# A radix-2 step in the channel transform of a fused attention and spectral-filter kernel

## The chip, the cores and the metric

The kernel runs on one core of one Trainium2 chip. The metric is the device time of one execution in microseconds (us).

## The reference

```python
x = A_x                                            # 1 x 2048 x 448, bf16
g = sigmoid((x * gate_w).sum(-1, keepdims=True))
q, k, v = heads(x @ A_wqkv)                        # 16 heads of 28
a = (softmax(q @ k.T * 28 ** -0.5) @ v) @ A_wo
X = rfft2(x)                                       # 2048 tokens x 225 frequencies
b = irfft2(X * (w_r + 1j * w_i))
out = g * a + (1 - g) * b
```

Both halves read A_x (B_x isn't used): attention over 16 heads, and a two-dimensional Fourier filter over tokens and channels. g mixes them for each token.

## The kernel before

**Attention.** Heads go in four groups of four; each head has a 32-row strip of the array. Queries are taken in four chunks of 512, so there are 16 (group, chunk) pairs, and 16 tiles of 128 keys each. A score matmul (K = 32 rows, 512 columns) gives one head's scores for one key tile. Two ways lead from there to the exponential. Most units go in pairs through psA or psB to ScalarE (L1032, 128x1024, 366 of them) into `ring`. The others (ND key tiles of each pair, 73 in all, four heads each) are done without ScalarE: VectorE turns the scores into the bit pattern of a bf16 power of two (L991, 292 of them, out of a `bg` bank into a `pd` tile), and GpSimd makes three more copies with shifted phase by an integer addition (L1001, INT64_ADD, 219 of them). Both kinds are then multiplied with the weighted values into the accumulator `pvb`, four matmuls side by side, one for each head (128x32 weights, 512 columns). There are nine `pd` tiles (NPD); one is free again when its `pvb` matmuls have read it.

**The spectral part** (`background`, L1249) is spread between the attention's instructions. Tokens are numbered so that partition p, tile t hold token 16p + t. Its stages:

- `fwd(t)` (L1269), 16 times: the channel transform of 128 tokens. The transposed tokens xT, in four chunks of channels (128, 128, 128, 65), are multiplied with the cosine and sine matrix Bd (450 columns: 225 frequencies, real and imaginary) into one `bg` bank, four accumulating matmuls, each split into four column tiles (`mm4`, L414). VectorE copies the bank to X1 (L1284).
- `fwd2(t)` (L1287): a 128-point transform over partitions with the matrix A, an eviction (L1296) and a DMA into the layout of the next stage (tile xtok, named UT there).
- `mid(g)`, 16 times (in `background`): the rest of the token transform as three `mm4` with the matrices CS (450, 225 and 225 columns), the product with the filter on VectorE (L1343 twice, then the two sums of SBUF tiles that give Z, L1348 and L1350), three `mm4` back and an eviction into UT (L1367).
- `inv(t)`, 16 times: a DMA brings the rows back to V2, four matmuls of 128 columns with A undo the 128-point transform, and VectorE multiplies with 1 - g, divided by g, into zt (L1388).
- `out_tile` (L1201) and `last_tile` (L1222), 16 together: one bank collects four `mm4` of the inverse channel transform (zt with Binv, which lies in Bd's tile, 448 columns each; rows of 225 frequencies in two pieces of 113, real and imaginary) and four `mm4` of the heads' output with `wo` (448 columns, in the tiles wpq and wpk). The eviction multiplies with g, and a DMA writes 128 tokens out. Four of these tiles come after the last exponential.

Projections of q, k and v (`proj_group`, `v_block`, `x_block`, `w_block`) are spread in the same way.

**What sets the order.** Every engine's instructions stand in one total order that is written out: the string TABLE holds, compressed, the number of each operation in the order of emission, with a second list that gives each use of a rotating bank one of three `bg` banks. `Sched.run` (L273) emits them so, and `pin` (L300) keeps that order on each engine. Numbers from 60000 on would be filler matmuls; this table has none. The planner's costs (the first arguments of `pe`, `dve`, `pool`) and due times are left in the code but decide nothing at run time.

**The shared port.** VectorE operations that take their operands from SBUF are marked `lk`: `ported` (L309) makes the next GpSimd instruction of the order wait for them. Of these are the squares of q and k (L745), the normalisation (L1176), Z (L1348, L1350) and the phase-weighted values (L886).

All matmuls are recorded under line 426, the helper `mm`; all DMAs under 401.

Of the kernel before, what the change touches and what calls it, by code (L numbers as in the profile page):

```python
# [13 lines left out]
BF16 = mybir.dt.bfloat16  # L14
# [8 lines left out]
F2 = 2 * F  # L23
NT, J, P = 16, 8, 128
FS, FN = (0, 112), 113
# [6 lines left out]
NPD, DKT = 9, 5  # L32
FILL0 = 60000
DUE_P = 4.0
TABLE = (
    "eNoN1oNyHloUQOF9tI//NGmjKqlt27Zt27Zt27Zt27Zt+95nWDPfLA1VAIBALAiFMGgAbSAcIiASPMSGOBAX4kF8iAID0dABEkBCSASJIQkk"
    "hWSggIKEFMAgAAhpIQTSgICaYKEGdIRsUB1SQUpIDtUgHaSHypAFUoOD7JADMkEGyAnBkBEyQ1YoBjEhBlSEXFAcSkApKA1BkB9KQm7IA4td"
    "GegNVaEcVIKy0ALyQj4oDF2gAMQk5aEg1IEKUAiKwBIXi4SSp1AUnkEYCScRpAdEktjkObyAl/AKXsMbiENyYC6MS+KRtxCfRJGcGE0SkIQk"
    "EXkHK2AlrILVsAbWQmKyDtZDT0hCJsBEmASTIQ/egSmwAWpDbtwId+Ee3IdNsBm2wFbYBtthB0yD6ZAXH8AMmAmzYDbMgbkwDx5CQ9jmdkJd"
    "mA8cFkAt2AULYREshkewBJZCE3gM+bAARrvd0BSewDJoBvlxDyyHvbAP3kNLSEoK4gf4CI1hP3SFA/AJPkM3KIKF8CDUhx1uKrSFwpiMJCeH"  # L40
    "oDmE6S9QFA9DCnIEjkJKUgyPwVcI1cXxG0wnM0gqMhBmkuNQCltDCUxNTkBJ7AxVSTUyi6Qh1UlprEHSklbQCU5CGUxH0pOyWJNkIBlJJlIO"
    "T8FpOANn4RychwtwEcrjbFIBs5Ih0B4yk2wkO8lBcpJc5DvkJpfgMuQhFTEvScAqYT6y012Bq5CfJGTXYLO7DgVIQVKIVMYbcBOykFtwG6pg"
    "YVKElCFVsSgpS4qRavgDfkJx8guSsepYAyN1claO1MTy5DdUILUwWtfGcB2b1cHYOg4bTerBH6iL9bAXJGIVyRiSmI0l3aE+jiOLXBLWAIEQ"
    "QgkjDXE84aQRCIJEEkU0aYTtIIIZ8g8sScoi2V9wxJPGGCBRLiULIk0wBqlEgklc3RTj62YYxkJICZJUN8d6rgVWJqVJfVeFtMSSpIFL58JZ"
    "K0zFGrrWmN41cnFZCtYGM7h4LLnO6NpiatYOM7lolky3x4Q6DUvPOmBCV4rUIolcYtcRM7BOGJ+lZUlcOtYZE+kumJEldVG6K8bR3bAwy8Qi"
    "dGLdA7tjEVacRbFcLIlOoXthT8zBEujemJul1CVYPJ2TZWF5WCqdl2VmfbAe6Yv1STbWD1Pr7KwBaUj6YyNSlBVjAzCrzqIHYkE2CAdjMZeV"
    "FXfZdCE2BEu42iSNHoql2DCsQwqwzDqHHo4lXSVWkpVyI7AuyalHYhFdhlVm5Vg+VpblZ6MwrS7N8uvRmFuPwfIsl07mxmJ1Ng6TuxRuPKZ0"
    "FdgEzKcL6YpsIg6CSZjKZdDpdTVWg2XXRfVknIKNSV3WjOXVefRULKanYQFdlU3Heqwzqc1mYBfSlczEOmwWdiNldEfWnczGOTgXm7PCuqCu"
    "yWqxediJldLNyXxsQRZgCV1aN2ELsSmrwhZhS9KKLMYl2IK1JvVZS1ZOl9QNWW63FNuyZdiOLcfiuqxegeV1PpdOr8T8rhHL41ZhLd2YFXAZ"
    "9Wos6Aq5NdiZdWFtWAW9FnuS+nod9mC9SD29HjfgUteEZNIbsQHrySrq3qSS3oR9yGasrWvoLdjMbcW+pClp7rZhe9bCdWD9SEO9HZuRlm4H"  # L50
    "9mOtXFPdn3VjO7GOHsx2YWvWWFfVNfVu3IN92BDWQu/F5ro768v2YWXdi/VmbUk7sh8P4EjWnoxiHchBbKlHQ0cylB3Cuno8tGKHsZw7gsNY"
    "XjecjWDlXQV3FHuQiu4YjmOdSCXXSY9lx7GBPoFDSRN9EgeyUziBTWSt9Wkcz7rqRrqLHkZSuzTuDJ7DtC6bG07O4giS3Y0kg1gOl9OdxwuY"
    "y61gK1l73ZVNJAPYJVzGLuJy1k5fxklkFWtDruBksppNIcPgKo5m1XQzPZWMYTPZNWylr2M3PYlNYTewg57FJrOp7Cb2J7ewmruNHXUbPYHM"
    "Z2NgALmDbfVdnM6quxlsAbuHS9hSVsPdx866pnuA3fVisoQsJcvIQ5zNlpNa7hH20EP1AD2NDNOD9BMcRR7jXDaHbWVVtGdj9Rj9FLexZ7ib"
    "bHF7yF6yj9wjz/E+eUAekmnsEZlD9pMD5CB5TJ6Qp+QQ6amfkcPkCHlOjpJjZAh5QQaRZe44mccC7AQ5SU6RV3iavMCXOFAvZCP1XDKPrCKL"
    "yGoyn6wga8hL8oqsJevIa1xPXpMNZCPZRHrpN6S6foNvyWayhWwl28hb3E52kJ3kHS4gi9l69o5M0EP0B9zMNrD3uIsMJMP1YP0Rt7A17BOu"
    "Y3tYZfcZp+sqbrT+govYATZO72UT9VdcyxaSwWQj+4bj3Cj9Hfvpg2y828T66Ml6gvuBp9lJdortZL/wDPuJQWy8HqEnuml6kvuN8/Qf3MeG"
    "ub84S//DXWw/286Gu91shAOZ2fUBIrO4wo7KHWyKzuqYPM4m6SLuBBvpRjkuhSzqrrC5+iqbqlHeZVJeYDP0RXaYHWFztJKz9T12iGlpZHxa"
    "2pVxvbWVR1kULetmaierOi9DWDQ9xubrleQsS0ADMiYLku1cQrpAx5DnWXtX29VxwfI+6+AesMEQIju6mPIS6+TW6FhyhV6pr7FQeYacJefI"
    "eRIm++rL7AK5SC6RyyRc3mbX2Tl2hVwl18gtdoddJzfITRIhb5HbJFLeIf3cKn2XxJY7dRy5UH8ii3R/956s13Flf/2KLdOvWTy51T1kA9xA"  # L60
    "FyUXuvhyg37Etuho2c19IAnkGzbIbdPLXUK53a3VS3UM9pEkki9Yd/eEvWQ3WA+XWPZ0SWRSeVC/Zb3cOv2ZJZPP2HO2Wm/VyWVd94WlkE/Z"
    "V7ZDT3Mp5WM23X1jN9kflkru0qnlDPeXpZGMz3Scz3KbdDqZVn5k79lm3dnt1enlUOjiMshP7DvbqD+wo3qJ/sEyykzyH9un37HMcrsG3tVl"
    "kYT/ZPt1Y5dVZpOGU75bW75HZ5f94Bc7pGOxHNLxnDKUHdCtXRP3m3mueC55TB/WuWWAa55HtnFBvK37TI7ovPK4jsklzye/kK8kv0ReQJ7Q"
    "sXgkD+EXdGx+TX8j30koLygLyWAexhO423q0Kywv6cR8jDupi8gRcEcXlVf1KZ2Ep+DFZAx+RV/UxWVKHs4juOAlZFM32I11l3VJGZ+Xkj9I"
    "PP5AP9ZD3GJdWkbxm7qMTMOf67IyLf9J4vKhrpyM5tf1L5KAl5cVZEL+myzXt3RFWUkm4ql4al5ZxuFJ+Sv9h1SR6fhf8lCf0VXlI93bpefV"
    "ZFZ+Qz/R1eU/0sfVkNl5X3dPJ+P3dU2ZmdeSL/RdnZzn4Nl4Jl5bznNZeB0529WVz/R8N8fVk6d1Ab7AFeSTXX2Zkc91b3QDOcXl5G/1WZ2Y"
    "NpS5eBKalE51yWgjmZxm4E1kEZ6bN5aF+GtdmL/U5zTQpzoPbyrz8WayKM/Pm0tC32lK3+vyvARvIRmtwFvKFe6DXulaSU5XudZyl1vtdjtB"
    "i/M17oduI/PytpKbdrIkF6a9LMX3uBAak8aiofSX3uv2uQ6ykwyjH/Unfdt1lP90BD2vI2kxHpvGoZ3lXx2XdpFlOTPlODVrXVfZTZbmSCUd"
    "Cftdd9lDluHrXGOu6EnXhGtqaE9ZhfeSv3Vvud590xtcH/lTV+Vf9UanjaV95QF32vWTm1xFXp834I7+0f3lKBgga/DK/K7zNIYJMwOlNDV5"
# [1370 lines left out]
```

## Time and profile before

| | |
|---|---|
| time, median of 3 runs | 384.12 us (384.02 to 384.2) |
| the profiled execution's own time | 384.64 us |
| its span | 382.8 us |
| granted TensorE clock | 0.999 |
| instructions | 12650 |

The span goes from the first to the last instruction; the time has 1.84 us around it. In rows of groups stand the line, engine, operation, tiles written and read, shapes and count, then busy time, mean duration in ns, and the idle time ahead of it with what ended it. In rows of a timeline stand start and duration in us and the count of merged instructions. In rows of stretches stand the stretch, its length, and the busy time of each engine with the number of instructions, then clock, DMA share and GB/s. PE is TensorE, PEld its weight loads, DVE VectorE, ACT ScalarE, POOL GpSimd.

### The profile page before, as it was taken

The page shows a single profiled execution, that of the slowest core. Times are in us where ns is not written, and L with a number is a line of the kernel's source. Part 1 is how long each engine was busy: PE and PEld are TensorE (multiplying, and loading weights), DVE is VectorE, ACT ScalarE, POOL GpSimd, SP SyncE. Part 2 cuts the span into 40 slices and gives each one's busy share as a digit, 9 for nine tenths or more (in the row PEclk, how much of TensorE's full clock was granted, in tenths as well). Part 3 has the DMA queues.
Part 4 walks back from the last instruction along what each step waited for, and adds up shares of the span by engine and source line. Part 5 has one row for each costly group of instructions (what it writes and reads, how often), then busy time and mean ns, then how long its engine had stood idle before and what let it go on. Part 6 is the DMA issues. An engine that isn't in the chain of part 4 may idle for free.

```text
span 382.8 us, 12650 instructions
## 1 busy us (share of the span) xinstructions
PE 375.9 (98%) x5140; PEld 140.7 (37%) x5141; DVE 333.4 (87%) x620; ACT 346.3 (90%) x381; POOL 247.3 (65%) x276
## 2 busy tenths in 40 slices
PE   8999999999999999999999999999999999999996
PEld 5643322233423222334434434333333333333444
DVE  1778977889899999999999999999999998878623
ACT  2699999999999999998996899999999999998861
POOL 5753874475764988647575594988769656564810
PEclk9999999999999999999999999999999999999999
DMA  8421010001112232222220132221323131122111
GB/s 228 101 58 52 4 33 2 21 25 21 22 40 48 70 130 61 53 44 71 48 65 10 30 70 47 76 57 23 82 51 82 53 97 44 46 64 64 48 57 63
DMA packets 31158, 21.68 MB, mean 57 GB/s; under 512 B 16260, under 2 KB 28796, under 8 KB 31100
## 3 DMA queue, kind: packets, MB, share of 16 engines
q1 hardware_dynamic: 29708, 20.41, 20.7%
q8 instruction: 40, 0.66, 0.7%
q10 hardware_dynamic: 1392, 0.46, 0.5%
q14 instruction: 18, 0.15, 0.1%
HBM read 14.97 MB, written 1.96 MB: 44 GB/s over the span
## 4 chain that ended last, share of the span: by engine, by line
PE 77%; DVE 9%; ACT 4%; DMA 3%; issue 2%; POOL 2%; SPq 1%; ACTq 0%; POOLq 0%; DVEq 0%
PE bg L426 31%; PE pvb L426 27%; PE psA L426 9%; PE psB L426 8%; ACT ring L1032 4%; DVE pd L991 4%; POOL pd L1001 2%; DMA X<-in_A_wqkv_dram 1%; PE bg L429 1%; DMA V<-xtok 1%; SPq L401 1%; DVE vw L864 1%; DMA Rb<-rsc 1%; DVE sq L745 1%; DMA wv<-in_gate_w_dram 1%
## 5 line engine op out<-in xcount | busy, mean ns | idle before, releaser
L1001 POOL INT64_ADD pd<-pd x219 | 224.8, 1041 | 98.8 <-DVE pd L991 23.6
L1032 ACT ACTIVATE ring<-psA 128x1024 bf16<-128x1024 f32 x183 | 192.5, 1052 | 13.0 <-PE psA L426 6.0
L991 DVE TENSOR_SCALAR pd<-bg 128x512 uint16<-128x512 f32 x292 | 190.3, 684 | 14.8 <-PE bg L426 4.7
L1032 ACT ACTIVATE ring<-psB 128x1024 bf16<-128x1024 f32 x183 | 192.5, 1052 | 5.0 <-PE psB L426 3.1
L426 PE MATMUL pvb<-pd,vd 128*32 128x512 bf16 x1168 | 102.0, 384 | 0.5 <-POOL pd L1001 0.2
L426 PE MATMUL bg<-q,k 32*128 32x512 bf16 x292 | 98.3, 383 | 0.4 <-DVE vt L877 0.3
L426 PEld LDWEIGHTS <-k 32*128 32x128 bf16 x1024 | 36.8, 91 | 117.9 <-issue 113.2
L426 PE MATMUL psA<-q,k 32*128 32x512 bf16 x366 | 71.9, 384 | 0.1
L426 PE MATMUL psB<-q,k 32*128 32x512 bf16 x366 | 71.4, 383 | 0.5 <-ACT ring L1032 0.4
L426 PE MATMUL pvb<-ring,vw 128*32 128x512 bf16 x732 | 66.7, 384 | 0.1
L426 PEld LDWEIGHTS <-vd 128*32 128x32 bf16 x1168 | 27.7, 94 | 37.3 <-issue 30.6
L426 PEld LDWEIGHTS <-vw 128*32 128x32 bf16 x732 | 17.7, 95 | 22.1 <-issue 17.4
L426 PEld LDWEIGHTS <-xT 128*128 128x128 bf16 (+3 forms) x512 | 19.3, 96 | 13.3 <-issue 11.7
L426 PE MATMUL bg<-Bd,xT 128*32 128x450 bf16 (+1 forms) x256 | 19.7, 358 | 0.0
L426 PE MATMUL bg<-xT,wpq 128*32 128x512 bf16 (+2 forms) x244 | 19.2, 382 | 0.0
L426 PE MATMUL bg<-xT,wpk 128*32 128x512 bf16 (+1 forms) x240 | 19.2, 383 | 0.0
L1343 DVE TENSOR_TENSOR t<-bg,Wg 128x450 bf16<-128x450 f32 x32 | 18.9, 618 | 0.1
L426 PE MATMUL bg<-Bd,X 113*32 113x448 bf16 x224 | 16.3, 355 | 0.0
L426 PE MATMUL bg<-wvr,xT 128*128 128x112 bf16 (+1 forms) x192 | 13.0, 213 | 0.0
L426 PEld LDWEIGHTS <-CS 128*32 128x32 bf16 x384 | 9.4, 95 | 8.7 <-issue 6.0
L1388 DVE TENSOR_TENSOR X<-bg,ogb 113x512 bf16<-113x512 f32 x16 | 10.7, 686 | 1.9 <-PE bg L426 1.7
L740 DVE TENSOR_SCALAR k<-bg 128x512 bf16<-128x512 f32 x15 | 10.3, 687 | 1.2 <-PE bg L426 1.2
(115 smaller groups left out, 297.6 us busy)
## 6 DMA issues: line engine op xcount, KB each, us to landing
Rb<-rsc SPq DMA_DIRECT2D x60, 64.0 KB
CS<-cCS SPq DMA_DIRECT2D x16, 192.0 KB
Wg<-in_B_w_i_dram SPq DMA_DIRECT2D x64, 28.1 KB
xtok<-Ab SPq DMA_DIRECT2D x16, 112.5 KB
V<-xtok SPq DMA_DIRECT2D x16, 112.5 KB
xtok<-in_A_x_dram SPq DMA_DIRECT2D x3, 448.0 KB
Wg<-in_B_w_r_dram SPq DMA_DIRECT2D x32, 28.1 KB
out_dram<-wpk SPq DMA_DIRECT2D x6, 112.0 KB
```

Source lines behind the costliest of these rows:

```text
L401: self.pin(e.dma_start(out=out() if callable(out) else out, in_=in_() if callable(in_) else in_))
L426: self.pin(self.nc.tensor.matmul(out, lhsT=lhsT, rhs=rhs, start=start, stop=stop, **kw))
L429: self.pin(self.nc.tensor.transpose(out=out, in_=in_, identity=self.c("ident")[0:n, 0:n]))
L740: self.pin(nc.vector.tensor_scalar(out=dst, in0=self.bgi(it), scalar1=SQ, scalar2=None, op0=ALU.mult))
L745: self.pin(nc.vector.tensor_tensor(out=sqs, in0=dst, in1=dst, op=ALU.mult))
L864: self.pin(nc.vector.tensor_tensor(out=free_dims(self.vw[g][:], [[128, nv], [32, 4], [1, DH]], 4 * b * 128), in0=src, in1=wv, op=ALU.mult))
L991: self.pin(nc.vector.tensor_scalar(out=ys[:, s, :].bitcast(U16), in0=self.bgi(it), scalar1=127 * UNITS, scalar2=0.0, op0=ALU.add, op1=ALU. ...
L1001: self.pin(nc.gpsimd.int64_add(out=fl(pds), in0=fl(ys), in1=PHASE[f] * 0x0001000100010001))
L1032: self.pin(nc.scalar.activation(out=self.ring[:, u0:u0 + len(st), :], in_=slot[:, 0:len(st), :], func=ACT.Exp, scale=LN2 / UNITS))
L1343: self.pin(nc.vector.tensor_tensor(out=out[:], in0=self.bgi(it)[:, 0:F2].rearrange("p (a f) -> p a f", a=2), in1=free_dims(Wg[:], [[F, 2], ...
L1388: self.pin(nc.vector.tensor_tensor(out=free_dims(self.zt[0:FN], [[128, 4], [1, 128]], 512 * t), in0=self.bgi(it)[0:FN, :].rearrange("p (a ...
```

## The change

A transform of 448 channels is split once into its even and odd channels: with E and O the transforms of the two, frequency f (0 to 112) is E + O, and frequency 224 - f is the conjugate of E - O (the twiddle factors lie in the odd matrix). The parts:

1. **Forward.** Channels come in chunks of 128 even, 128 odd, 96 even and 97 odd (the last one has the row of ones). Bd has 2 x 113 columns. `fwd` has four `mm4` of 226 columns in place of 450, even chunks into one half of the bank, odd ones into the other. The eviction has 452 columns. Then two GpSimd operations, `lo` (2 x 113 elements, sums) and `hi` (2 x 112, differences, output walked backwards), make the 450 columns in one of three new tiles Xs, from which `fwd2` reads.
2. **Middle.** After Z, two GpSimd operations (226 elements each, the second input walked backwards) make sums and differences in Zs, which are the first two Xs tiles; the three `mm4` back take these (452, 226 and 226 columns).
3. **Inverse.** Rows of 452 in UT and V2, four pieces of 113; `out_mm` has four `mm4` of 224 columns in place of 448, two for the even and two for the odd output channels, into the halves of the bank.
4. **What follows from it.** `wo` is read in steps of two, so that its columns land in the same halves; the last evictions write in steps of two; the transposes read tokens in steps of two; the loads of wqkv and of gate_w are cut into 256 and 192 rows (384 and 64 before), with the copies that spread them; two evictions of a later token block become one.
5. **A new order** of all 3679 operations (3618 before), with two fillers. ND, RING, NPD and all other numbers of the attention are as before.

```diff
 def fwd(t):
             for c in range(4):
-                n = 128 if c < 3 else 65
+                n = CH[c]
...
-                    self.mm4(self.bgi(it)[:, 0:F2], self.xT[t // 4][0:n, c, 128 * (t % 4):128 * (t % 4) + 128],
+                    h = 2 * NE * (c % 2)
+                    self.mm4(self.bgi(it)[:, h:h + 2 * NE], self.xT[t // 4][0:n, c, 128 * (t % 4):128 * (t % 4) + 128],
                              self.Bd[0:n, c, :], c == 0, c == 3)
...
-            x1.append(self.dve(.54, lambda: self.pin(nc.vector.tensor_copy(
-                out=self.X1[:, t, 0:F2], in_=self.bgi(it)[:, 0:F2])), ops[-1:] + pads, k, free=it))
+            e = self.dve(.54, lambda: self.pin(nc.vector.tensor_copy(
+                out=self.X1[:, t, 0:F4], in_=self.bgi(it)[:, 0:F4])), ops[-1:] + pads, k, free=it)
+            b, xs = self.X1[:, t, :], self.Xs[t % NXS]
+            def lo():
+                self.pin(nc.gpsimd.tensor_tensor(out=free_dims(xs[:], [[F, 2], [1, NE]]), in0=free_dims(b, [[NE, 2], [1, NE]]),
+                                                 in1=free_dims(b, [[NE, 2], [1, NE]], 2 * NE), op=ALU.add))
+            def hi():
+                self.pin(nc.gpsimd.tensor_tensor(out=free_dims(xs[:], [[F, 2], [-1, NE - 1]], F - 1),
+                                                 in0=free_dims(b, [[3 * NE, 2], [1, NE - 1]]),
+                                                 in1=free_dims(b, [[-NE, 2], [1, NE - 1]], 2 * NE), op=ALU.subtract))
+            x1.append([self.pool(.6, f, [e, xr[t % NXS]], k) for f in (lo, hi)])
...
-            m = self.pe(450, lambda: self.mm4(self.bgi(it2)[:, 0:F2], self.A[:, 0, :], self.X1[:, t, 0:F2], True, True),
-                        [x1[t], dA], k2, mode="col", rel=k2 - W, acq=it2)
+            m = self.pe(450, lambda: self.mm4(self.bgi(it2)[:, 0:F2], self.A[:, 0, :], self.Xs[t % NXS][:, 0:F2], True, True),
+                        x1[t] + [dA], k2, mode="col", rel=k2 - W, acq=it2)
+            xr[t % NXS] = m
...
+            zs = self.Zs[i]
+            def zc(dif, Z=Z, zs=zs):
+                self.pin(nc.gpsimd.tensor_tensor(
+                    out=zs[:, 2 * NE * dif:2 * NE * dif + 2 * NE].rearrange("p (a f) -> p a f", a=2), in0=Z[:, :, 0:NE],
+                    in1=free_dims(Z[:], [[F, 2], [-1, NE]], F - 1), op=ALU.subtract if dif else ALU.add))
+            zc2 = [self.pool(.6, lambda d=d, zc=zc: zc(d), [z1, z2, pr[i]], k) for d in range(2)]
+            prz[i], prt[i] = [z1, z2], zc2
...
     def out_mm(self, t, k, bank, start, stop):
         if k < 4:
-            self.mm4(bank, self.zt[0:FN, t, 128 * k:128 * k + 128], free_dims(self.Binv[0:FN], [[1, D]], k * D), start, stop)
+            h = D // 2 * (k in (1, 2))
+            self.mm4(bank[:, h:h + D // 2], self.zt[0:FN, t, 128 * k:128 * k + 128],
+                     free_dims(self.Binv[0:FN], [[1, D // 2]], k * (D // 2)), start, stop)
         else:
             g = k - 4
-            self.mm4(bank, self.q[g][:, 128 * t:128 * t + 128], self.wo_pad[g], start, stop)
+            self.mm4(bank, self.q[g][:, 128 * t:128 * t + 128], free_dims(self.wo_pad[g], [[1, 2], [2, D // 2]]), start, stop)
...
-            out=fin, in0=self.bgi(it)[:, 0:D], scalar1=self.glog[:, t:t + 1], scalar2=None, op0=ALU.mult)),
+            out=free_dims(fin, [[1, 2], [2, D // 2]]), in0=self.runs(self.bgi(it)), scalar1=self.glog[:, t:t + 1], scalar2=None, op0=ALU.mult)),
...
+    def xch(self, t, c, n):
+        return free_dims(self.xtok[:], [[2, n]], F4 * t + 256 * (c // 2) + c % 2)
```

Here F = 225, F2 = 450, F4 = 452, NE = 113, NXS = 3, D = 448 and CH = (128, 128, 96, 97).

More of the change, by code (lines that the diff above doesn't have):

```diff
@@ L32 @@
 NPD, DKT = 9, 5
+NXS = 3
 FILL0 = 60000
@@ L41 @@
[L41 to L45, printed above, removed]
@@ L1364, in background, with b1, half, b2 @@
[L1364 to L1366 removed]
+            def b1(it2=it2, CS=CS, zs=zs):
+                self.mm4(self.bgi(it2)[:, 0:F4], CS[:, 3, :], zs[:], True, False)
+            def half(o):
+                return [[2 * NE, 2], [1, NE]], NE * o
+            def b2(it2=it2, CS=CS, zs=zs):
+                self.mm4(free_dims(self.bgi(it2), *half(0)), CS[:, 4, :], free_dims(zs[:], *half(1)), False, False)
@@ L1367, in background, with b3 @@
+            def b3(it2=it2, CS=CS, zs=zs):
+                self.mm4(free_dims(self.bgi(it2), *half(1)), CS[:, 5, :], free_dims(zs[:], *half(0)), False, True)
+            for fn, nn in ((b1, 452), (b2, 226), (b3, 226)):
+                ops2.append(self.pe(nn, fn, zc2 + dl[:1] + ops2[-1:], k, mode="col", acq=it2 if not ops2 else None))
+            pr[i] = ops2[-1]
             vev.append(self.dve(.54, lambda it2=it2, g=g: self.pin(nc.vector.tensor_copy(
-                out=self.UT[:, g, 0:F2], in_=self.bgi(it2)[:, 0:F2])), [ops2[-1], ops[-1]], k, free=it2))
+                out=self.UT[:, g, 0:F4], in_=self.bgi(it2)[:, 0:F4])), [ops2[-1], ops[-1]], k, free=it2))
```

300 lines of the change are left out of this document (149 added, 151 removed).

## The prediction

> **What bounds the kernel now.** I read the page's shares and its chain first, then the busy times by stage, then rows of single operations.
>
> ```profile
> PE 375.9 (98%) x5140; PEld 140.7 (37%) x5141; DVE 333.4 (87%) x620; ACT 346.3 (90%) x381; POOL 247.3 (65%) x276
> PE 77%; DVE 9%; ACT 4%; DMA 3%; issue 2%; POOL 2%; SPq 1%; ACTq 0%; POOLq 0%; DVEq 0%
> ```
>
> TensorE is busy for 98% of the span and holds 77% of the chain that ended last. A busy PE need not be a full one, so I look at who it waits for (from 20 to 372 us, the whole answer):
>
> ```profile
> PE bg L426 <- DMA V<-xtok: 0.4, 1, 0.4
> PE psB L426 <- ACT ring L1032: 0.4, 2, 0.2
> PE bg L426 <- DVE vt L877: 0.3, 1, 0.3
> PE pvb L426 <- POOL pd L1001: 0.2, 1, 0.2
> ```
>
> It waits 1.3 us in 352. Its instruction stream is the bound. The busy times by stage, with cuts at the first and last instructions of the spectral parts (columns: PE, weight loads, DVE, ACT, POOL):
>
> ```profile
> 36.00:129.20 93.20, 93.16 (x1249) 29.41 (x1250) 82.85 (x150) 91.54 (x102) 58.63 (x61) 1.00 0.11 28
> 129.20:157.00 27.80, 27.80 (x375) 8.25 (x373) 27.41 (x49) 27.48 (x31) 24.14 (x24) 1.00 0.30 88
> 157.00:301.00 144.00, 143.20 (x1967) 52.55 (x1964) 142.64 (x281) 136.53 (x149) 102.59 (x103) 1.00 0.23 51
> 301.00:314.00 13.00, 12.75 (x152) 5.11 (x148) 12.32 (x20) 12.95 (x15) 7.58 (x9) 1.00 0.31 97
> 314.00:371.00 57.00, 56.58 (x865) 22.12 (x866) 41.76 (x68) 51.06 (x55) 34.06 (x34) 1.00 0.17 53
> ```
>
> 36 to 129 is the forward channel transform (`fwd`), 157 to 301 the middle (`mid`), 314 to 371 the output tiles. The clock is 1.00 throughout. ACT is right behind PE. How far behind show two of its exponentials that follow each other without a gap:
>
> ```profile
> 245.55 1.10 ACT L1032 ACTIVATE ring<-psA 128x1024 bf16<-128x1024 f32 x1
> 246.45 1.12 ACT L1032 ACTIVATE ring<-psB 128x1024 bf16<-128x1024 f32 x1
> 12.81 1.02 ACT L1032 ACTIVATE ring<-psA 128x1024 bf16<-128x1024 f32 x1 [1.72 <-PE psA L426]
> 370.60 1.02 ACT L1032 ACTIVATE ring<-psB 128x1024 bf16<-128x1024 f32 x1
> ```
>
> They start 0.90 us apart; 366 of them need 329.4 us, and from the first start to the last end there are 358.8. So ACT has 29 us to spare over the run, more than the change can take from PE.
>
> **What the change takes from PE.** A four-tile matmul (`mm4`) of the forward channel transform has 226 columns in place of 450, one of the inverse 224 in place of 448. The rows that price them:
>
> ```profile
> 345.60 0.94 PE L426 MATMUL bg<-Bd,X 113*32 113x448 bf16 x16
> 346.37 0.36 PE L426 MATMUL bg<-wpq,q 128*32 128x448 bf16 x4
> 160.14 0.27 PE L426 MATMUL bg<-xtok,CS 128*32 128x225 bf16 x4
> 160.24 1.04 PE L426 MATMUL bg<-xT,wpq 128*32 128x512 bf16 x16
> ```
>
> Four `mm4` of 448 columns (16 matmuls) hold PE for 0.77 us, 0.193 each; one of 225 holds it for 0.10. So 0.095 us is saved on each. The counts:
>
> ```profile
> L426 PE MATMUL bg<-Bd,xT 128*32 128x450 bf16 x192 | 15.3, 358 | 0.0
> L426 PE MATMUL bg<-Bd,xT 65*32 65x450 bf16 x64 | 5.9, 356 | 0.0
> L426 PE MATMUL bg<-Bd,X 113*32 113x448 bf16 x204 | 15.0, 355 | 0.0
> ```
>
> Forward: 256 matmuls, 64 `mm4`, 6.1 us, all from 36 to 129. Inverse: the third row is for 314 to 371, 51 `mm4`, 4.8 us. The other 13 run at the end; most of them stand there while PE waits for the last normalisation, so I count only the last four, 0.4 us. Full price: 10.9 us before 371 and 0.4 after it.
>
> **What it adds to GpSimd.** Two tensor_tensor operations per `fwd` and two per `mid`, 64 in all, each of 226 elements per partition with two inputs. This operation is in no row. The nearest:
>
> ```profile
> L525 POOL COPY wpq<-X 128x336 bf16<-128x336 bf16 x3 | 1.4, 464 | 1.6 <-DVE sq L745 1.6
> L528 POOL COPY wpq<-X 64x112 bf16<-64x112 bf16 x3 | 0.8, 275 | 4.7 <-DVE sq L745 4.6
> L1001 POOL INT64_ADD pd<-pd x219 | 224.8, 1041 | 98.8 <-DVE pd L991 23.6
> ```
>
> The two copies differ by 224 elements and 189 ns: 0.84 ns an element and 0.18 us fixed. Lower end: a copy of 226, 0.37 us. Upper end: a whole INT64_ADD, 1.04 us. Two reads at the copy's rate give 0.56; the INT64_ADD, (1.04 - 0.18) / 512 = 1.68 ns for an element, gives the same. One input or the output is walked in steps and backwards, so I take 0.60: 38.4 us (23.7 to 66.6).
>
> [...] No run here shows the operation yet.
>
> Does that fit? GpSimd also stands aside for VectorE operations that take SBUF operands (marked `lk` in the kernel: GpSimd's next instruction waits for them). Their time from 36 to 371, for L745, L1176, L1348, L1350 and L886, and from 129.2 to 157 for the first two, the only ones there:
>
> ```profile
> 36.00:371.00 335.00, 10.44 (x26) 1.00 0.20 50
> 36.00:371.00 335.00, 9.78 (x14) 1.00 0.20 50
> 36.00:371.00 335.00, 4.69 (x16) 1.00 0.20 50
> 36.00:371.00 335.00, 4.46 (x16) 1.00 0.20 50
> 36.00:371.00 335.00, 6.82 (x16) 1.00 0.20 50
> 129.20:157.00 27.80, 0.84 (x2) 1.00 0.30 88
> 129.20:157.00 27.80, 0.68 (x1) 1.00 0.30 88
> ```
>
> That is 36.2 us beside GpSimd's own 227.0 in the five stages: 263.2 of 335, 79%. In the densest stage, 129 to 157, it is 24.14 + 1.52 of 27.8: 92%, and PE did not wait. With 38.4 added there are 301.6 us of work, which at 92.3% take 326.8: GpSimd lets this stretch shrink by 8.2 us, where PE would let it shrink by 10.9. So GpSimd and the port, not PE, set the gain.
>
> Locally it is worse: the middle has 102.6 + 22.2 (of those 36.2) + 19.2 = 144.0 us for a stage of 144. It can't stay there at 92%; it has to stretch by 12 us into the stages behind it, where GpSimd is busy for 60%, and the output tiles wait for its last result. I take 3 us off for that. Below nothing I have no reason to go, as `mid` gets longer in its chain (VectorE's Z, then GpSimd, then PE) and nothing gets shorter; the upper end is the 12 us.
>
> **New waits.** PE's second forward matmul waits for two GpSimd operations in place of an eviction, the middle's second set for two more. Behind it on PE stands everything in order, scores and so ACT included; PE's 1.3 us of waits leave no cover, only the order's distance between producer and reader does. On GpSimd the additions stand in one queue with the `pd` phases, whose readers are PE's `pvb` matmuls.
>
> **Costed at nothing.** Two evictions of each later token block become one; I count no gain for three instructions. Two filler matmuls in the order are a fraction of a microsecond. Rows of 452 elements for 450 (evictions, transfers to and from the 16-row layout): 2 columns each. The weights' loads have the same rows and number of DMAs, split 256 + 192 for 384 + 64. Bd and Binv move half the bytes, far ahead of use. The last evictions write bf16 in steps of two, from PSUM at the same count. Reading `wo` in steps of two as moving operand has no row: nothing if a step costs nothing, +0.19 us on each of 64 `mm4` (12 us) if it halves the rate. I take nothing, as the transposes' stepped loads are as unknown and nothing in the trace speaks for the loss; the 12 us stay as a rival.
>
> [...]
>
> **The sum.** From 36 to 371: 8.2 allowed by GpSimd, less 3.0 for the crowded middle: -5.2. The end: -0.4. The profiled execution took 384.64 us (span 382.8); that makes 379.0. The median of the runs shown, 384.12, is 0.5 below the profiled one, so the forecast is **378.5**.
>
> **Rivals.** *GpSimd becomes the bound, and the kernel slower.* At 0.72 us an operation (335 x 0.923 - 263.2 = 46.0, over 64) nothing of the stretch's gain is left, before the crowding. At 0.80 it is 314.4 / 0.923 = 340.6: +5.6, with 3 for the crowding and -0.4 at the end +8.2, **392.3**. For it: the sum above, and
>
> ```profile
> L1348 DVE TENSOR_TENSOR Z<-t x16: 268/276/600, 164.3 to 299.6; 128x225 bf16<-128x225 bf16 x16
> ```
>
> where one Z took 600 ns for 276: it met a GpSimd operation and stood still. Against it: GpSimd idles for 98.8 us ahead of its INT64_ADDs, and only part of that is the port.
>
> [...]
>
> *PE gets all of it.* If an operation costs 0.56 or less and the middle spreads, GpSimd allows 11.1, and PE sets the end again: 384.64 - 11.3 - 0.5 = **372.8**. For it: 0.56 is what the rows give without my supplement. Against it: ACT has 1.7 us idle from 36 to 129, so the forward gain has to be used further back, where DVE is at 99%.
>
> *The stepped operand halves the rate of the `wo` matmuls.* +12 on the forecast's -5.6: **390.5**, slower. That the narrower `mm4` don't take half the time is hardly a case: 0.10 us is in the trace.
>
> **Chances.** The forecast's own case, 376 to 383.3: 0.38. All of it, below 376: 0.20. Within 0.2% of 384.12 (about what a measurement can tell): 0.07. GpSimd as the bound, slower: 0.28. Stepped operand: 0.05, other waits of the new order: 0.02, both slower. So faster 0.58, same 0.07, slower 0.35. The faster case's own range is 372.5 to 383; the one that should hold 8 in 10 goes from 372.5, just under the full gain, to 392, the price of the slower rival: it leaves out some 0.05 below and 0.13 above.
>
> **What would show it.** Right: `Bd` matmuls 0.10 us apart; tensor_tensor at 0.55 to 0.65; GpSimd's busy time near 285 us; PE's waits for POOL below 3 us. Wrong: PE or ACT idle with POOL as releaser in 157 to 301, Z much longer than 276 ns, `wpq,q` matmuls wider apart than 0.19. A tensor_tensor above 0.7 us alone would break the sum.

## The result, and the profile after

The changed kernel takes **927.37 us** (924.64 to 928.56, four runs) against 384.16 (384.02 to 384.85): a ratio of 2.412, 95% interval 2.406 to 2.419. The forecast was 378.5, the range 372.5 to 392. The loss is 543 us.

The page of the kernel after: the shares, and two rows of the slices.

```profile
PE 472.1 (51%) x5149; PEld 149.9 (16%) x5149; DVE 346.0 (37%) x617; ACT 361.0 (39%) x381; POOL 283.1 (31%) x340
PE   9941416930543534324722647377525335163998
PEclk9965657965765665555755677565856557565999
```

No engine is busy for more than 51% of the span. Before, TensorE stood at 98%. So no engine has too much to do; they wait. For whom TensorE waits from 20 to 920 us (us in total, times, longest):

```profile
PE pvb L434 <- POOL pd L1005: 298.5, 35, 39.5
PE bg L434 <- POOL Xs L1377: 99.9, 12, 18.6
PE bg L434 <- POOL Xs L1299: 25.1, 3, 15.5
PE bg L434 <- POOL Xs L1303: 21.6, 4, 5.9
```

445 us of waits, all for GpSimd; before, they were 1.3 us from 20 to 372. But GpSimd itself is busy for only 283.1 us, 31%. Its groups in the page say what it does in the rest:

```profile
L1005 POOL INT64_ADD pd<-pd x219 | 224.9, 1037 | 299.5 <-issue 225.3
L1377 POOL TENSOR_TENSOR Xs<-Z 128x226 bf16<-128x226 bf16 x32 | 18.2, 581 | 144.4 <-issue 130.1
L1303 POOL TENSOR_TENSOR Xs<-X 128x224 bf16<-128x224 bf16 x16 | 8.9, 557 | 84.6 <-issue 70.8
L1299 POOL TENSOR_TENSOR Xs<-X 128x226 bf16<-128x226 bf16 x16 | 8.9, 559 | 78.6 <-issue 64.6
```

The operations are as short as they were expected to be: an INT64_ADD takes 1037 ns (1041 before), a tensor_tensor 557 to 581. The idle time ahead of them is ended by "issue", that is, by nothing that the profile shows: 490.8 us in the four rows. Before, the INT64_ADDs had 98.8 us of idle time ahead of them, and its largest part was put down to VectorE. A stretch of GpSimd's timeline shows where the idle time sits (start, duration, idle time before in brackets):

```profile
299.58 4.08 POOL L1005 INT64_ADD pd<-pd  x4
310.77 0.56 POOL L1303 TENSOR_TENSOR Xs<-X 128x224 bf16<-128x224 bf16 x1 [7.12 <-issue]
317.27 2.05 POOL L1005 INT64_ADD pd<-pd  x2 [5.95 <-issue]
326.58 0.55 POOL L1299 TENSOR_TENSOR Xs<-X 128x226 bf16<-128x226 bf16 x1 [7.25 <-issue]
333.24 3.07 POOL L1005 INT64_ADD pd<-pd  x3 [6.11 <-issue]
343.49 0.55 POOL L1299 TENSOR_TENSOR Xs<-X 128x226 bf16<-128x226 bf16 x1 [7.18 <-issue]
```

Each time GpSimd goes from INT64_ADD to tensor_tensor, about 7 us pass, and about 6 on the way back; between two of a kind none do. The sequencer's rows of the four lines name what stands there, an instruction that the page counts in no group (POOLq is GpSimd's sequencer; count, duration in ns, first and last start):

```profile
L1005 POOLq MODIFY_POOL_CONFIG  x88: 1/1/11, 32.7 to 848.3; - x88
L1299 POOLq MODIFY_POOL_CONFIG  x22: 1/1/11, 75.4 to 415.4; - x22
L1303 POOLq MODIFY_POOL_CONFIG  x24: 1/1/11, 44.4 to 432.8; - x24
L1377 POOLq MODIFY_POOL_CONFIG  x40: 1/1/11, 459.2 to 839.9; - x40
```

They come in pairs: 43 pairs ahead of a tensor_tensor, 44 ahead of an INT64_ADD. Before, there was one pair:

```profile
L1001 POOLq MODIFY_POOL_CONFIG  x2: 4/4/4, 33.8 to 33.9; - x2
```

Over the whole trace of after, a tensor_tensor starts 7.1 us behind its pair (median of 43, 6.76 to 7.47), an INT64_ADD 5.7 us (median of 43, 5.55 to 6.12). The first pair of the execution, at 32.7 us, is left out: the INT64_ADD starts 1.8 us behind it, and waits for VectorE meanwhile. 43 x (7.1 + 5.7) = **550 us**, against a loss of 543. What GpSimd does in these stops no row says. The trace shows them at all 86 changes between the two kinds, 43 each way.

**Theory:** each change between INT64_ADD and tensor_tensor stops GpSimd for 6 to 7 us, and TensorE, in its fixed order, stops with it. **Rivals:** the additions are too much work for GpSimd; the new order is bad; the rest of the change (narrow matmuls, stepped operands) is bad.

### The profile page after: what moved, and what is told of

It is laid out like the page before. It is cut to its first block, busy times and chain, and to the rows that moved or that the text cites. A ratio compares the mean times of both kernels' runs of the same rounds, so it can differ in the third digit from the quotient of the medians.

```text
span 924.5 us, 12895 instructions
## 1 busy us (share of the span) xinstructions
PE 472.1 (51%) x5149; PEld 149.9 (16%) x5149; DVE 346.0 (37%) x617; ACT 361.0 (39%) x381; POOL 283.1 (31%) x340
## 5 line engine op out<-in xcount | busy, mean ns | idle before, releaser
L1005 POOL INT64_ADD pd<-pd x219 | 224.9, 1037 | 299.5 <-issue 225.3
L434 PE MATMUL pvb<-pd,vd 128*32 128x512 bf16 x1168 | 132.8, 488 | 298.8 <-POOL pd L1005 298.5
L434 PE MATMUL bg<-q,k 32*128 32x512 bf16 x292 | 126.0, 489 | 0.8 <-DVE pd L995 0.4
L434 PE MATMUL psB<-q,k 32*128 32x512 bf16 x366 | 87.7, 467 | 0.6 <-ACT ring L1036 0.2
L434 PE MATMUL psA<-q,k 32*128 32x512 bf16 x366 | 87.7, 465 | 0.1
L434 PE MATMUL pvb<-ring,vw 128*32 128x512 bf16 x732 | 84.2, 477 | 0.1
L434 PE MATMUL bg<-Xs,CS 128*32 128x226 bf16 (+1 forms) x192 | 16.8, 439 | 99.9 <-POOL Xs L1377 99.9
L1377 POOL TENSOR_TENSOR Xs<-Z 128x226 bf16<-128x226 bf16 x32 | 18.2, 581 | 144.4 <-issue 130.1
L434 PE MATMUL bg<-xT,wpq 128*32 128x512 bf16 (+3 forms) x244 | 24.2, 452 | 0.6 <-DVE wpq L532 0.6
L434 PE MATMUL bg<-xT,wpk 128*32 128x512 bf16 (+2 forms) x240 | 23.6, 462 | 0.0
L434 PEld LDWEIGHTS <-xT 128*128 128x128 bf16 (+5 forms) x512 | 20.9, 104 | 15.0 <-issue 14.6
```

The source lines that it names most:

```text
L434: self.pin(self.nc.tensor.matmul(out, lhsT=lhsT, rhs=rhs, start=start, stop=stop, **kw))
L1005: self.pin(nc.gpsimd.int64_add(out=fl(pds), in0=fl(ys), in1=PHASE[f] * 0x0001000100010001))
L1377: self.pin(nc.gpsimd.tensor_tensor(out=zs[:, 2 * NE * dif:2 * NE * dif + 2 * NE].rearrange("p (a f) -> p a f", a=2), in0=Z[:, :, 0:NE], in ...
```

## Experiments

**e1, the change without changes of type.** In the changed kernel, INT64_ADD becomes a copy of the same bytes, which leaves out the phase shift:

```diff
-                    fl = lambda t: t[:].rearrange("p a b -> p (a b)").bitcast(U64)
-                    self.pin(nc.gpsimd.int64_add(out=fl(pds), in0=fl(ys), in1=PHASE[f] * 0x0001000100010001))
+                    fl = lambda t: t[:].rearrange("p a b -> p (a b)").bitcast(F32)
+                    self.pin(nc.gpsimd.tensor_copy(out=fl(pds), in_=fl(ys)))
```

> The changed kernel with each of the 219 integer additions on GpSimd (INT64_ADD, 1.03 us) replaced by a GpSimd copy of the same tile, seen as 1024 fp32 elements (about 1.04 us by the rate of the small copies): the phase shift of the power-of-two copies is left out. The 64 tensor_tensor operations stay on GpSimd. Theory (switch): GpSimd pays 5.7 to 7.1 us each time it goes from an INT64_ADD to a tensor_tensor or back, and copies need no such change: 372 to 382 us. Rival (load): the 64 operations themselves overbook GpSimd and the port it shares with VectorE: GpSimd has as much work as before, so still above 800 us. Rival (order): the new order is bad whatever stands in it: still far above 400.

380.26 us (380.11 to 380.8), ratio to before 0.989 (0.987 to 0.991). Its page, GpSimd's groups, and all that TensorE waits for from 20 to 371 us:

```profile
PE 371.6 (98%) x5149; PEld 140.4 (37%) x5149; DVE 334.0 (88%) x617; ACT 346.4 (91%) x381; POOL 276.9 (73%) x340
```

```profile
L1005 POOL COPY pd<-pd 128x1024 f32<-128x1024 f32 x219 | 221.5, 1043 | 55.1 <-DVE pd L995 23.1 <-PE pvb L434 8.6 <-DVE q L1180 7.6
L1377 POOL TENSOR_TENSOR Xs<-Z 128x226 bf16<-128x226 bf16 x32 | 18.5, 590 | 8.7 <-DVE Z L1372 5.0 <-DVE Z L1370 2.4 <-DVE q L1180 0.8
```

```profile
PE bg L434 <- DVE pd L995: 0.8, 3, 0.4
PE pvb L434 <- DVE pvs L1168: 0.3, 1, 0.3
PE psB L434 <- ACT ring L1036: 0.2, 1, 0.2
```

The copy takes 1043 ns, as INT64_ADD did; the 64 tensor_tensor are all still there, on GpSimd, in the new order; "issue" is gone, and with it 547 us. GpSimd goes 84 times from a copy to a tensor_tensor or back, with a median of 0.0 us between them, and has one MODIFY_POOL_CONFIG pair in all. It has the work and is not late with it. The load, the order and the narrow matmuls fall as causes.

**e2, the additions on VectorE.** The 64 tensor_tensor go to VectorE (marked `lk`), in the places of the order where GpSimd had them:

```diff
...
-                self.pin(nc.gpsimd.tensor_tensor(
+                self.pin(nc.vector.tensor_tensor(
...
```

> The changed kernel with its 64 sums and differences on VectorE in place of GpSimd, nothing else changed, order included. Theory (switch): no tensor_tensor is left on GpSimd, so no switch: VectorE has 64 times 0.2 to 0.3 us more, 13 to 19 us, in stages where it is near its limit; 376 to 394 us. Rival (load): relief of GpSimd also helps, but by 64 times 0.56 = 36 us of its time only: above 800. Rival (order): above 400.

396.99 us (396.55 to 398.05), ratio 1.033 (1.031 to 1.035), 3 above the expected span. Without tensor_tensor on GpSimd the 543 us are gone here too; a loss of 12.4 remains. GpSimd's waits for the additions:

```profile
POOL pd L1005 <- DVE Xs L1377: 20.0, 11, 3.0
POOL pd L1005 <- DVE Xs L1303: 11.7, 7, 3.6
POOL pd L1005 <- DVE Xs L1299: 8.6, 5, 4.8
```

VectorE's additions of SBUF tiles stop GpSimd's INT64_ADDs for 40.3 us through the `lk` waits, and VectorE itself had next to no room in the middle (busy for 142.6 of 144 us before). That this makes the 12.4 us is argued, not shown.

**e3 and e4, eight additions in the kernel before, apart and in a row.** Into the old kernel, whose GpSimd has no tensor_tensor, go eight of 226 elements with unused output: in e3 one at a time, 24 INT64_ADDs apart, in e4 all behind the 116th.

```diff
+                    if self.nadd in range(20, 212, 24):
+                        for _ in range(1):
+                            self.pin(nc.gpsimd.tensor_tensor(out=self.dmy[:], in0=self.zero[:, 0:226],
+                                                             in1=self.zero[:, 0:226], op=ALU.add))
```

> The kernel before, with eight extra tensor_tensor operations on GpSimd (226 elements of a zeroed tile into a scratch tile that nobody reads), each alone behind an INT64_ADD, 24 additions apart. Theory (switch): 8 times 7.1 + 5.7 = 102 us of GpSimd time, of which the idle time around each takes some: 450 to 490 us. Rival (load): 8 times 0.56 = 4.5 us, hidden or nearly: 384 to 389 us.

> The kernel before, with the same eight extra tensor_tensor operations on GpSimd, but all in one row behind one INT64_ADD. Theory (switch): one pair of switches, 12.8 us, and 4.5 us for the eight: 390 to 402 us, some 70 us or more under the eight that stand apart. Rival (load): the same as the eight that stand apart, within 3 us.

e3: **502.78 us**, 118 more, 14.8 for each addition. e4: **403.29**, 18.7 more for all eight. (One run each; before 384.56.) Both are above their expected spans, e3 by 13 us and e4 by 1. The mean granted clock was 0.877 in e3 and 0.974 in e4; how much of the excess the clock makes was not separated. GpSimd's waits in e3:

```profile
POOL dmy L1006 <- issue: 49.6, 7, 7.3
POOL pd L1002 <- issue: 47.5, 8, 6.1
```

GpSimd's timeline in e4:

```profile
225.89 5.05 POOL L1006 TENSOR_TENSOR dmy<-zero 128x226 bf16<-128x226 bf16 x8 [7.17 <-issue]
230.88 0.46 POOL L816 CAST vw<-w 128x64 bf16<-128x64 f32 x1
236.92 3.18 POOL L1002 INT64_ADD pd<-pd  x3 [5.57 <-issue]
```

The same eight operations, 4.5 us of work, cost 118 or 18.7 us: what counts is how often GpSimd goes there and back, once in e4 and eight times in e3. The CAST that follows the eight waits for nothing.

**e5, the control of e1.** The kernel before with the same copies.

```diff
-                    fl = lambda t: t[:].rearrange("p a b -> p (a b)").bitcast(U64)
-                    self.pin(nc.gpsimd.int64_add(out=fl(pds), in0=fl(ys), in1=PHASE[f] * 0x0001000100010001))
+                    fl = lambda t: t[:].rearrange("p a b -> p (a b)").bitcast(F32)
+                    self.pin(nc.gpsimd.tensor_copy(out=fl(pds), in_=fl(ys)))
```

> The kernel before, with its 219 INT64_ADDs done as GpSimd copies of 128x1024 f32, as in e1 (so the phase shift is left out). It is the control of e1. Theory (without switches the rest of the change is worth the 4.3 us of e1): a copy takes 1.04 us as INT64_ADD does, so this kernel stays at 384.6, between 383.8 and 385.4, and e1's gain belongs to the narrower matmuls. Rival (the copies themselves are lighter, on the port or on GpSimd, and give e1's gain): about 380.3.

383.37 us (382.89 to 383.93), ratio 0.998 (0.997 to 0.999): the copies are worth some 0.8 us themselves, just under the expected span. So what the change gains where nothing switches is 383.37 - 380.26 = **3.1 us**, not 4.3 (3.5 if each is taken against the kernel before in its own round, 384.56 for e1 and 384.21 for e5).

**e6, which types switch.** Eight small operations apart, as in e3, but three copies, three tensor_scalars and two memsets.

```diff
...
+                    if self.nadd in (20, 44, 68):
+                        self.pin(nc.gpsimd.tensor_copy(out=self.dmy[:], in_=self.zero[:, 0:226]))
+                    if self.nadd in (92, 116, 140):
+                        self.pin(nc.gpsimd.tensor_scalar(out=self.dmy[:], in0=self.zero[:, 0:226], scalar1=2.0, scalar2=None, op0=ALU.mult))
+                    if self.nadd in (164, 188):
+                        self.pin(nc.gpsimd.memset(self.dmy[:], 0.0))
```

> The kernel before, with eight small operations of 226 elements put one at a time into GpSimd's queue of INT64_ADDs, far apart: three copies, three tensor_scalars, two memsets; their output is not used. Theory (a switch belongs to some types of operation, not to every change of type): the copies and memsets cost their own 0.2 to 0.4 us each; before's own copies and memsets stand between INT64_ADDs without a pause. If tensor_scalar belongs with tensor_tensor, each of the three costs 14.8 us as an isolated tensor_tensor did: 384.6 + 44 = 429, with three issue waits of about 7 us ahead of them and three of about 6 behind. Rival (every type but copy and memset is at home with INT64_ADD, and tensor_tensor is special): 385 to 386. Rival (any change of type costs): 384.6 + 8 x 14.8 = 503.

429.26 us (one run, before 384.21): 45 more, 15.0 for each tensor_scalar. The groups of GpSimd in e6:

```profile
L1002 POOL INT64_ADD pd<-pd x219 | 224.9, 1041 | 117.6 <-DVE pd L992 24.7 <-issue 17.4 <-DVE sq L746 14.3
L1007 POOL TENSOR_SCALAR dmy<-zero 128x226 bf16<-128x226 bf16 x3 | 2.5, 833 | 21.9 <-issue 21.9
L1005 POOL COPY dmy<-zero 128x226 bf16<-128x226 bf16 x3 | 1.1, 375 | 0.0
```

Three stops of 7.3 us ahead of the tensor_scalars, three of 5.8 behind them, none at the copies. The memsets have none either. So tensor_scalar pays as tensor_tensor does; copy, cast and memset paid nothing beside INT64_ADD, and none of them paid behind a tensor_tensor (e1, e3, e4). That fits a class of operations, not each change of type. Whether GpSimd stops between a tensor_scalar and a tensor_tensor too was not tried.

**e7, the forward split alone, its sums on TensorE.** In the order of before; `fwd2` adds the halves in its own bank, by four narrow groups in place of one wide one. The chunks of channels, the stepped transposes and the split loads of the change come with it.

```diff
...
-            m = self.pe(450, lambda: self.mm4(self.bgi(it2)[:, 0:F2], self.A[:, 0, :], self.X1[:, t, 0:F2], True, True),
+            def four():
+                o, x = self.bgi(it2), self.X1[:, t, :]
+                self.mm4(free_dims(o, [[F, 2], [1, NE]]), self.A[:, 0, :], free_dims(x, [[NE, 2], [1, NE]]), True, False)
+                self.mm4(free_dims(o, [[F, 2], [1, NE]]), self.A[:, 0, :], free_dims(x, [[NE, 2], [1, NE]], 2 * NE), False, False)
...
```

> Forward split only, in the order of before: four matmuls of 226 columns in place of 450, and the sums and differences are made by TensorE inside the second forward transform (four groups of 226 and 224 columns with A and -A in place of one of 450); nothing is added to GpSimd or VectorE; the inverse is as before. Theory (TensorE bounds, a narrowed group of four column tiles saves 0.095 us): 64 x 0.095 = 6.1 us less, 16 x 2 x 0.097 = 3.1 us more, so 3.0 us less: 381.6, between 381 and 382.7. Rival (ACT and VectorE, both at 98% and 89% in the forward stretch, do not let TensorE run ahead there): 384 to 385.

387.93 us (387.31 to 390.57), ratio 1.011 (1.008 to 1.013): slower, where 3 us less was expected; even the rival was too low. TensorE's time on the matmuls that read A, in the two stretches 36 to 129.2 and 129.2 to 157, before and in e7:

```profile
36.00:129.20 93.20, 2.56 (x28) 1.00 0.11 28
129.20:157.00 27.80, 3.30 (x36) 1.00 0.30 88
```

```profile
36.00:129.20 93.20, 3.99 (x112) 1.00 0.12 27
129.20:157.00 27.80, 5.14 (x144) 1.00 0.28 83
```

ScalarE's exponentials (tile `ring`) in the same stretches, before and in e7:

```profile
36.00:129.20 93.20, 91.54 (x100) 1.00 0.11 28
129.20:157.00 27.80, 27.48 (x31) 1.00 0.30 88
```

```profile
36.00:129.20 93.20, 91.63 (x100) 1.00 0.12 27
129.20:157.00 27.80, 26.93 (x29) 1.00 0.28 83
```

From 36 to 129 the wide groups became cheap, and exactly as many exponentials (100) were done. ScalarE is busy for 98% there, which would make it the bound beside TensorE and void the gain; no run frees it, so this is argued. From 129 to 157, where TensorE is full, the added groups cost 1.84 us, and two exponentials fewer are done. The cost lies in a stretch where it is paid, the gain in one where it is not. Counted along ScalarE's 366 exponentials, the profiled execution of e7 is 2.5 us behind that of before at number 160 and still at 240, and 3.5 at 310; what adds the last 1.0 is not known.

**e8, both splits in the old order, the inverse sums on VectorE.**

```diff
...
+            def zz(t34=t34, Z=Z, zc=zc):
+                self.pin(nc.vector.tensor_tensor(out=Z[:, 1, :], in0=t34[:, 0, :], in1=t34[:, 1, :], op=ALU.add))
+                zc(0)
+                zc(1)
...
```

> As e7, and the inverse split too, with its 32 sums and differences on VectorE behind Z, in the order of before. TensorE has 3.0 + 4.8 + 0.4 = 8.2 us less. VectorE has 32 more operations of 0.3 to 0.4 us, 11 us, all in the middle stretch, where it is busy for 142.6 of 144 us. Theory (an operation costs what its engine has no room for): the middle stretches by about 11 us, of which the lighter TensorE work there gives back nothing: 384.6 - 8.2 + 11 = 387.4, between 384 and 391. Rival (VectorE's operations in the middle can be put off into the stretch behind it, where it is busy for 73%): 377 to 381.

395.42 us (395.17 to 395.84), ratio 1.029 (1.028 to 1.030). (In some of its steps the additions stand ahead of Z's real half and read an older one; their number and size are as told.) The theory had the sign and missed the size by 8 us. It falls behind steadily through the middle, from 1.0 us at exponential 100 to 11.0 at 300. e7's 3.7 us of loss, which the sum had as a gain of 3.0, would make 6.7 of these 8.

**e9 and e10, the inverse split alone, its sums late on VectorE.** The sums are made from the rows that come back per token tile, after the middle, 10 or 16 operations ahead of their readers.

```diff
...
+            def sums(t=t, v2=v2):
+                vs = vsb[t % 4]
+                for dif in range(2):
+                    self.pin(nc.vector.tensor_tensor(
+                        out=free_dims(vs, [[NE, 2], [1, NE]], 2 * NE * dif), in0=free_dims(v2[:], [[F, 2], [1, NE]]),
+                        in1=free_dims(v2[:], [[F, 2], [-1, NE]], F - 1), op=ALU.subtract if dif else ALU.add))
...
```

> Inverse split only, in the order of before, forward as before. The sums and differences are made late: not behind Z in the middle, but from the rows that come back for each token tile (tile V2), by two VectorE operations of 226 elements per tile, placed ten operations of the order ahead of the four matmuls that read them. GpSimd gets nothing, so there is no change of operation type on it. Theory (a narrowed group of four matmuls saves 0.095 us wherever TensorE bounds, and VectorE has room from 301 to 371, where it is busy for 54 of 70 us): 51 x 0.095 = 4.8 us and 0.4 at the end, less 64 stepped wo groups at 0.012 = 0.8: 379.8 to 382. Rival (the 32 additions, 10 to 12 us, hold up VectorE's pd units, and the wait for the transfer now stands in VectorE's queue): 385 to 390.

> As e9, with the additions sixteen operations of the order ahead in place of ten. If in e9 TensorE waits for the additions, this is faster by that wait; if VectorE waits for the transfer at the head of its queue, it is slower by about 0.6 us for each tile that comes late. Otherwise the same as e9 within 1 us.

e9: 389.89 us (389.41 to 393.1), ratio 1.014 (1.012 to 1.016), within the rival's span; e10: 392.95 (one run, so not to be told from e9's highest). The profiled execution of e9 took 392.94 us at a mean clock of 0.981. Up to 303 us it does not differ from before; at 371 it is 8.3 us behind. Stretches of 3 us of it (busy time of PE, PEld, DVE, ACT, POOL, then the granted clock):

```profile
304.00:307.00 3.00, 1.97 (x25) 1.11 (x16) 2.80 (x8) 2.12 (x3) 0.83 (x2) 1.00 0.47 131
307.00:310.00 3.00, 3.00 (x28) 1.06 (x25) 3.00 (x7) 2.55 (x3) 1.49 (x2) 0.67 0.30 88
310.00:313.00 3.00, 3.00 (x21) 0.85 (x21) 2.18 (x7) 1.84 (x3) 1.84 (x2) 0.50 0.27 89
313.00:316.00 3.00, 3.00 (x32) 1.06 (x31) 2.44 (x6) 2.02 (x3) 0.21 (x1) 0.69 0.20 61
...
322.00:325.00 3.00, 1.65 (x24) 0.82 (x16) 2.74 (x9) 2.12 (x3) 1.20 (x2) 1.00 0.15 44
325.00:328.00 3.00, 3.00 (x23) 0.97 (x22) 1.12 (x2) 1.44 (x2) 0.88 (x1) 0.51 0.02 3
328.00:331.00 3.00, 3.00 (x26) 0.64 (x25) 2.21 (x5) 1.92 (x3) 1.04 (x1) 0.50 0.00 0
```

Twice TensorE idles, for 1.0 and 1.35 us within 3, and behind each the granted clock is about half for 6 to 7 us. But only two of the six executions had the low clock (392.94 and 393.1 us, both at 0.981). The other four, at 0.998 to 1.000, took 389.41 to 389.93, and are 5.3 to 5.8 us slower than before all the same. So the halved clock makes some 3 us of the 8.3, and most of e9's loss is not the clock's. No execution of e9 at full clock was profiled.

**e11 and e12, the transfers sooner, and filler matmuls where TensorE waits.**

```diff
+            pd = min(at[d.i], max(p - 44, n0, ps[t - 3] + 1 if t > 2 else 0))
...
-FILLS = (0, 0)
+FILLS = (10, 8)
```

> As e9 (inverse split alone, sums late on VectorE), with the transfers of V2 issued up to 44 operations of the order earlier (a V2 tile is free as soon as its sums are made) and the sums fourteen operations ahead of their matmuls where the transfer allows it. In e9 the 8.3 us were lost in two places, 3.7 from 304 to 311 and 4.2 from 318 to 326, each a wait of TensorE of 1 to 2 us followed by 6 us at a granted clock of 0.50. Theory (the second wait comes from sums that stand too late, and its cost is mostly the clock): the second place goes away, the first (tiles 0 and 1, whose rows can't come sooner) stays: 384.1 + 3.7 - 3 for the narrower matmuls behind it, 383 to 387. Rival (the additions on VectorE cost the time, not the waits): 389 to 391 as e9.

> As e11, with 18 idle groups of four matmuls of 256 columns of zeros (added to an accumulator, so they change nothing) ahead of the inverse matmuls of tiles 0 and 1, where TensorE waits in e9. They are 1.9 us of work for nothing. Theory (a wait of 1 us costs 3 us more through the halved clock behind it): the clock stays at 1.00 and this is 2 to 3 us faster than e11. Rival (the clock has another reason, or the wait itself is the cost): the same as e11, or slower by up to 1.9 us.

e11: 389.58 us (388.66 to 392.12), ratio 1.015 (1.012 to 1.019). e12: 390.39 (389.44 to 391.06), 1.016 (1.014 to 1.017). (In both, the sums of three tiles stand behind the matmuls that read them.) e11 meets its rival's span, 389 to 391. Its second place lost 0.7 us in place of 4.2, yet the median stays: its six executions fall into three at a clock of 1.00 or 0.998 (388.66 to 388.84) and three at 0.986 to 0.991 (390.32 to 392.12). At full clock it is 0.9 us ahead of e9. The stretches of e12:

```profile
304.00:307.00 3.00, 2.93 (x66) 1.72 (x66) 2.27 (x7) 2.54 (x3) 1.26 (x2) 1.00 0.41 120
307.00:310.00 3.00, 3.00 (x57) 1.58 (x56) 2.68 (x7) 1.19 (x2) 1.27 (x2) 1.00 0.34 96
310.00:313.00 3.00, 2.83 (x31) 1.38 (x28) 3.00 (x8) 3.00 (x4) 1.67 (x3) 1.00 0.16 55
```

With the filler the clock stays at 1.00 in the place where it halved, and e12's executions stand at 0.994 to 1.000. But it is not faster than e11 in the median: at exponential 310 its profiled execution is 2.7 us behind where it was at 300, that of e11 4.0, so a loss of 4.0 was traded for one of 2.7. The theory "2 to 3 us faster" falls; e11's own executions differ by up to 3.4 us with the clock. The profiled e12, at a clock of 1.00, is 4.7 us behind at the last exponential: 2.7 from that place, and 1.5 between numbers 340 and 345, where TensorE waits 0.6 us each for a `pd` of VectorE and one of GpSimd; e9 and e11 lose 1.2 and 1.5 there too. That fits e9's rival, additions that hold up the `pd` units. Why the narrower matmuls give nothing back in the output tiles stays open. No version here that keeps the integer additions beats the kernel before.

## Why the prediction was wrong

**The step that failed is "What it adds to GpSimd".** It priced 64 operations by their durations, "38.4 us (23.7 to 66.6)", and took that for the whole cost. The durations were right: 0.56 to 0.58 us for 0.60. GpSimd's busy time was right: 283.1 us for "near 285". The missing term was not an operation but the way between two types: 43 times 12.8 us, 550 us. With it an addition costs not 0.60 us but 9.2 on average (36 + 550 over 64). e1 and e2 take the term away from two sides, e3, e4 and e6 put it into the old kernel by itself.

**Could it be seen before?** The old trace had one MODIFY_POOL_CONFIG pair, at 33.8 us, and the first INT64_ADD came 0.6 us later, so the trace priced the pair at nothing. That pair has no tensor_tensor ahead of it in its own execution. In e1 the only pair stands ahead of the first tensor_tensor, which starts 0.1 us behind it. So the first pair of an execution was cheap for either of the two. In every trace here that has one, it stands ahead of the type that the kernel also ends with; whether the two have to do with each other wasn't tried. The old GpSimd mixed INT64_ADD freely with copies, casts and memsets, and that looked like proof that types mix. The bounds of the unknown operation were taken from below by a copy and from above by INT64_ADD, "nearest rows" of one operation; neither holds what lies between operations. The prediction weighed how long this operation takes, and nothing that comes ahead of it. Three of its four signs of being right came true (matmuls 0.10 us apart, tensor_tensor at 0.55 to 0.65, GpSimd busy for near 285 us); all three are durations. The fourth, TensorE's waits for GpSimd below 3 us, was the one that could see this cost: 445.

**What bounds the kernel.** Right for before. After, it is nobody's work but GpSimd's stops.

**What the change takes from PE.** Right in size: four-tile groups of 226 columns start 0.10 to 0.11 us after each other in e1 and e7, those of 450 0.20 before (medians over the trace). Where it can be taken was only half seen. The forecast named ScalarE's 1.7 us of idle time from 36 to 129 as a reason against the full gain; in e7, in the old order, nothing of the forward gain arrived there.

**GpSimd's density and the crowded middle.** e1 is, but for its copies, the kernel that the forecast described. It is ahead of before by 2.6 us at exponential 160, by 0.3 at 260 and by 3.6 at the last. So the middle took back 2.3 us, for which 3.0 had been set, and gave it back later (3.0 against its control e5, which is 0.7 ahead of before at 260). That the size fits is luck: 3.0 was a choice between nothing and 12, set for a GpSimd that is late, and in e1 TensorE waits for GpSimd nowhere from 20 to 371. That also answers the forecast's new waits: there are none. Of the port that the forecast names, the trace of before shows this: of the 32 sums that give Z (L1348, L1350), the 27 that ran beside no GpSimd operation took 266 to 292 ns, one with 59 ns beside an INT64_ADD took 274, and the four with 176 to 468 ns beside one took 309 to 600. The net against the control is 3.1 us, where 5.6 had been forecast.

**Stepped `wo` operand.** Neither nothing nor 12 us: four-tile groups on `wo` stand 0.202 us apart in e1, 0.189 before (medians), which is 0.8 us over 64.

**The rivals.** "GpSimd becomes the bound" had the right engine and sign, by a wrong mechanism (operations of 0.72 us or more) and a price of 8 us for 543. "PE gets all of it" is out by e1. The chance of slower, 0.35, rested mostly on that rival (0.28); the range of 8 in 10 ended at its price, with no room for a cost that no row of operations could show.

## What to carry to other kernels

Before an operation of a new type is put on GpSimd, ask what its queue holds, and count how often the type would change; here a visit costs some 13 us (7.1 + 5.7), or 15 where it stands alone (e3), and eight operations in one visit cost little more than one (18.7 us in e4). Copies, casts and memsets were free company here (no stop ahead of them in e4 and e6); tensor_tensor and tensor_scalar beside INT64_ADD were not (7.1 and 5.7 us, 7.3 and 5.8). When idle time is ended by "issue" and every duration is as expected, look at the sequencer's instructions between the operations. And a saving counts in the stretch where it falls: in e7 it fell where ScalarE was nearly full (98% busy), and its cost where TensorE was (27.8 of 27.8 us before).

## What the runs showed of the hardware

A short wait of TensorE can cost more than itself. In e9's profiled execution 1.0 us idle within 3 us was followed by a clock of 0.50 to 0.69 for 6 to 7 us, and it fell 4.0 us behind there, between exponentials 300 and 310. Further on, 1.35 us idle within 3 us was followed by 0.50 to 0.51.

But such a wait need not cost it. Later in the trace of e11, 0.9 us idle within 3 us is followed by a clock of 1.00:

```profile
328.00:331.00 3.00, 2.10 (x29) 0.81 (x21) 3.00 (x9) 2.69 (x4) 2.23 (x3) 1.00 0.33 110
331.00:345.00 14.00, 13.66 (x223) 5.56 (x219) 11.01 (x19) 12.51 (x14) 8.30 (x9) 1.00 0.17 53
```

In e2 TensorE idles for up to 1.25 us within 3 us (158 to 161), and the clock is 1.00 from 36 to 385. The same kernel is hit in one execution and not in another: e11 ran at 388.7 us with a clock of 1.00 and at 392.1 with 0.986. What decides it, the runs don't show. In the kernel after, the mean clock of 0.673 comes with the stops: its `pvb` matmuls on `pd` take 488 ns each, 384 before.
